# Down projection of a fused Hyena filter and gated layer with the tokens held in the array and the weights moving

## The chip, the cores and the metric

The kernel runs on one core of a Trainium2 chip. The metric is the device time of one execution in microseconds (us); lower is better. About 0.2% (7.5 us) is what a measurement of this kernel can tell from no change.

## The reference

Everything is float32. A long convolution of each of 128 channels over 12480 positions is followed by a layer on 49920 tokens of width 128 with 2048 hidden units:

```
u = x * v                                   # (4, 12480, 128)
h_filt = (relu(pos_emb @ w1) @ w2) * exp(-0.01 * pos)[:, None]
y = causal convolution of u with h_filt, channel by channel (rfft, product, irfft)
z = (x * y).reshape(49920, 128)
h = z @ w_in                                # (49920, 2048)
g = h * cos(h)
return g @ w_out                            # (49920, 128)
```

The change lies in the last line, `g @ w_out`, the down projection, whose inner size is 2048.

## The kernel before

The convolution is done as a transform in two factors, 96 by 120, with matmuls against tables (the lines L407, L448, L479 and L504 are its four kinds of matmul). It leaves z in DRAM in rows of four tokens. The gated layer (named "moe" in the code) takes z back in tiles `n` of up to 128 rows, so of up to 512 tokens: there are 98 tiles, the first with 104 rows, the last with 88, the 96 between with 128. Each tile goes through 16 pieces `c` of 128 hidden units.

One step `(n, c)` has these parts. `moe_up` (L743) multiplies piece `c` of `w_in`, held in the array, with the tile's 512 tokens as the moving operand, into a PSUM bank `ph` of which there are four. ACT (L746), DVE (L749), POOL (L752), ACT (L757) and DVE (L759) turn `ph` into `gt = h * cos(h)`, laid out with the 128 hidden units on the partitions and the 512 tokens along the row. `moe_down` (L768) multiplies piece `c` of `w_out`, held in the array, with `gt` as the moving operand, and adds into the bank `acc`, whose rows are the 128 output features. After piece 15 `moe_evict` copies `acc` to `ot` (L774, on ACT). Since the sums stand with features on the partitions, `moe_back` turns them with four transposes on TensorE (L126, through a `ph` bank) and copies the result to `ob` (L783, on ACT), and `moe_store` issues the DMAs to the output from SP's queue (L794). `moe_turn` does the same kind of four transposes on the way in, from `zb` to `at` (L126, L737).

The order of all of it is written out by hand in one loop. In iteration `i`, which is step `(n, c)`, the loop issues the up projection of step `i`, the down projection of step `i - 4` (`LAG = 4`), the evict if that was a piece 15, the second half of the gating of step `i - 1`, and then by the value of `c`: the turn of the next tile at `c = 3`, the way back of the tile before at `c = 8`, its store at `c = 10`. After that it issues as many units of the next batch's convolution as are owed, so that the convolutions of batches 1 to 3 and the last part of batch 0's lie between the steps; at about 3000 us there is no convolution left and the steps stand alone.

For reading the trace: every float32 matmul that is no transpose appears as two weight loads and two matmul records, so a step's up projection is "x2" and its down projection is "x2". A transpose appears as one weight load and one matmul record.

Of the kernel before, what the change touches and what calls it, by code (L numbers as in the profile page):

```python
# [9 lines left out]
F32 = mybir.dt.float32  # L10
# [6 lines left out]
P = 128  # L17
BANK = 512
# [12 lines left out]
def kernel(  # L31
# [46 lines left out]
    nc = tc.nc  # L78

    B, S, D = x.shape  # L80
# [18 lines left out]
    NFC = DFF // P  # L99
    G = BANK // D  # L100
    UA = 2
# [4 lines left out]
    LAG = 4  # L106
# [17 lines left out]
    def transpose(dst, src, ident):  # L124
        n = src.shape[0]
        nc.tensor.transpose(dst, src, ident[0:n, 0:n])  # L126
# [241 lines left out]
    def n2s(g):  # L368

        a = g * UA  # L370
        return [*range(a, a + UA), *range(N2 - UA - a, N2 - a)]
# [344 lines left out]
    ats, accs = {}, {}  # L716

    def first_row(n):
        return min(R + (n - 1) * P, NROWS) if n else 0

    def rows_of(n):
        return first_row(n + 1) - first_row(n)
# [7 lines left out]
    def moe_turn(pool, n):  # L730
        m = rows_of(n)
        zb = zbs.pop(n)
        pt = ps_h.tile([P, BANK], F32, name="ph")
        for i in range(G):
            transpose(pt[:, i * m:(i + 1) * m], zb[0:m, i, :], ident)
        at = pool.tile([D, BANK], F32, name="at")
        nc.scalar.copy(out=at[:, 0:G * m], in_=pt[:, 0:G * m])  # L737
        ats[n] = at

    def moe_up(pool, n, c):  # L740
        m = G * rows_of(n)
        ph = ps_h.tile([P, BANK], F32, name="ph")
        nc.tensor.matmul(ph[:, 0:m], w_in_sb[:, c * P:(c + 1) * P], ats[n][:, 0:m],  # L743
                         start=True, stop=True)
        a = pool.tile([P, BANK], F32, name="a", bufs=3)
        nc.scalar.activation(a[:, 0:m], ph[:, 0:m], AF.Identity,  # L746
                             bias=quarter[:, 0:1], scale=INV_TWO_PI)
        k = pool.tile([P, BANK], F32, name="k")
        nc.vector.tensor_scalar(out=k[:, 0:m], in0=a[:, 0:m], scalar1=ROUND,  # L749
                                scalar2=ROUND, op0=ALU.add, op1=ALU.subtract)  # L750
        f = pool.tile([P, BANK], F32, name="f")
        nc.gpsimd.tensor_tensor(f[:, 0:m], a[:, 0:m], k[:, 0:m], op=ALU.subtract)  # L752
        return ph, f, m

    def moe_act(pool, ph, f, m):
        cs = pool.tile([P, BANK], F32, name="cs")
        nc.scalar.activation(cs[:, 0:m], f[:, 0:m], AF.Sin, scale=TWO_PI)  # L757
        gt = pool.tile([P, BANK], F32, name="gt", bufs=4)
        nc.vector.tensor_tensor(gt[:, 0:m], ph[:, 0:m], cs[:, 0:m], op=ALU.mult)  # L759
        return gt  # L760

    def moe_down(n, c, gt):
        if c == 0:

            accs[n] = bank() if made[0] == B * NG and n % 2 else \
                ps_acc.tile([P, BANK], F32, name="acc")
        m = G * rows_of(n)
        nc.tensor.matmul(accs[n][:, 0:m], w_out_sb[:, c, :], gt[:, 0:m],  # L768
                         start=(c == 0), stop=(c == NFC - 1))

    def moe_evict(pool, n):
        m = G * rows_of(n)
        ot = pool.tile([D, BANK], F32, name="ot", bufs=1)
        nc.scalar.copy(out=ot[:, 0:m], in_=accs.pop(n)[:, 0:m])  # L774
        return ot

    def moe_back(pool, n, ot):
        m = rows_of(n)
        pt = ps_h.tile([P, BANK], F32, name="ph")
        for i in range(G):  # L780
            transpose(pt[0:m, i * D:(i + 1) * D], ot[:, i * m:(i + 1) * m], ident)
        ob = pool.tile([P, 2, UA * D], F32, name="ob", bufs=1)
        nc.scalar.copy(out=ob[0:m, :, :].rearrange("p h n -> p (h n)"), in_=pt[0:m, :])  # L783
        return ob

    def moe_store(n, ob):
        row = first_row(n)
        while row < first_row(n + 1):
            b, g, n1 = row // R // NG, row // R % NG, row % R
            count = min(R - n1, first_row(n + 1) - row)  # L790
            first, _, second, _ = n2s(g)
            start = out[b * S + n1 * N2 + first, :]
            at = row - first_row(n)
            nc.sync.dma_start(  # L794
                bass.AP(tensor=start.tensor, offset=start.offset,
                        ap=[[N2 * D, count], [(second - first) * D, 2], [1, UA * D]]),
                ob[at:at + count, :, :])
            row += count

    with tc.manual_schedule():  # L800
        with tc.tile_pool(name="psum", bufs=8, space=PSUM) as psum, \
                ExitStack() as first:
            def bank():
                return psum.tile([P, BANK], F32, name="ps")
# [11 lines left out]
            with tc.tile_pool(name="layers", bufs=1, side="right") as pool:  # L816
# [14 lines left out]
                ident = pool.tile([P, P], F32, name="ident")  # L831
# [68 lines left out]
            ident = wpool.tile([P, P], F32, name="ident")  # L900
            make_identity(nc, ident)
            w_in_sb = wpool.tile([D, DFF], F32, name="w_in_sb")
            w_out_sb = wpool.tile([P, NFC, D], F32, name="w_out_sb")
# [6 lines left out]
        ps_h = ctx.enter_context(tc.tile_pool(name="ps_h", bufs=4, space=PSUM))  # L910
# [9 lines left out]
        mpool = ctx.enter_context(tc.tile_pool(name="moe", bufs=2))  # L920
# [18 lines left out]
        def load(n):  # L939
            while made[0] * R < first_row(n + 1):  # L940
                next(conv)
            moe_load(mpool, n)
# [2 lines left out]
            next(conv)  # L945
        moe_turn(mpool, 0)
        steps = [(n, c) for n in range(NALL) for c in range(NFC)]
        hidden, gates, ots, obs = {}, {}, {}, {}
        for i in range(len(steps) + LAG):
            if i < len(steps):  # L950
                n, c = steps[i]
                if n == 0 and c == NFC // 2:
                    load(1)
                if c == NFC - 4 and n + 2 < NALL:
                    load(n + 2)
                hidden[i] = moe_up(mpool, n, c)
            if i >= LAG:
                pn, pc = steps[i - LAG]
                moe_down(pn, pc, gates.pop(i - LAG))
                if pc == NFC - 1:  # L960
                    ots[pn] = moe_evict(mpool, pn)
            if 0 <= i - 1 < len(steps):
                gates[i - 1] = moe_act(mpool, *hidden.pop(i - 1))
            if i < len(steps):

                if c == (LAG - 1 if n else NFC - 2) and n + 1 < NALL:
                    moe_turn(mpool, n + 1)
                if c == NFC // 2 and n - 1 in ots:
                    obs[n - 1] = moe_back(mpool, n - 1, ots.pop(n - 1))
                if c == NFC // 2 + 2 and n - 1 in obs:  # L970
                    moe_store(n - 1, obs.pop(n - 1))
            owed += 1.0
            while owed > 0.0:
                owed -= next(conv, owed)
        for n in sorted(ots):
            moe_store(n, moe_back(mpool, n, ots[n]))
# [1 line left out]
_INS = ['x', 'v', 'pos_emb', 'w1', 'w2', 'moe_w_in', 'moe_w_out']  # L978
_OUTS = [((49920, 128), 'float32')]
# [25 lines left out]
```

## Time and profile before

| what | value |
|---|---|
| median of 3 runs | 3759.47 us (3757.68 to 3761.73) |
| profiled execution: span | 3758.9 us |
| instructions in the span | 47177 |
| mean granted TensorE clock | 0.995 |
| PE busy, matmuls | 3690.6 us, 98% of the span, 13546 records |
| PE weight loads (PEld), beside the matmuls | 2110.4 us, 56% |
| DVE, ACT, POOL busy | 74%, 67%, 68% |

The profiled execution's span lies 0.6 us below the median of the runs, within their spread. In the trace an operation is named by engine, line and tiles, as `acc<-gt,w_out_sb 128*128 128x512` for a matmul that writes `acc`, has a stationary operand of 128 by 128 and a moving one of 128 by 512. Matmul and weight-load records have modelled ends that include the way through the array, so that successive records overlap: how long one occupies TensorE is read from the distance between successive starts, not from a record's length.

### The profile page before, as it was taken

Reading aid. Unit: us, or ns where it says so; the run is one execution under the profiler, and the core shown is the slowest. Engines: PE = TensorE matmul, PEld = TensorE weight load, DVE = VectorE, ACT = ScalarE, POOL = GpSimd, SP = SyncE. Lnnn points to the kernel's source line nnn. Section 1 sums busy time; section 2 is a strip of 40 time slices with the busy share of each in tenths; the row PEclk is TensorE's granted clock in tenths of the full one; section 3 lists DMA queues with packets and bytes.
Section 4 is the critical chain, followed back from the end, with each engine's and each line's share of the span. In section 5 each row is a group of like instructions: output and inputs, shape, how many; then the busy total and the mean of one; then the engine's idle time right before and its main releaser. Section 6 shows DMA issues by size and latency. Waiting matters only on the chain.

```text
span 3758.9 us, 47177 instructions
## 1 busy us (share of the span) xinstructions
PE 3690.6 (98%) x13546; PEld 2110.4 (56%) x13546; DVE 2773.7 (74%) x5586; ACT 2508.2 (67%) x4660; POOL 2557.6 (68%) x2318
## 2 busy tenths in 40 slices
PE   7898999999999999999999999999999999999999
PEld 6777555555566556555565556555566544444444
DVE  8887997687866787788766776788765666666666
ACT  5757776766665557766665567666664677777777
POOL 6666776588845665688745664788644677777776
PEclk9999999999999999999999999999999999999999
DMA  6263551022203650122104530122105200000000
GB/s 167 64 185 107 155 167 33 25 72 79 72 12 91 181 151 12 40 79 77 52 18 128 180 105 21 52 79 76 38 21 172 76 23 17 17 23 18 17 23 13
DMA packets 209499, 276.14 MB, mean 73 GB/s; under 512 B 17111, under 2 KB 146535, under 8 KB 209111
## 3 DMA queue, kind: packets, MB, share of 16 engines
q1 hardware_dynamic: 209239, 273.12, 24.8%
q8 instruction: 109, 1.79, 0.2%
q14 instruction: 151, 1.24, 0.1%
HBM read 193.64 MB, written 79.42 MB: 73 GB/s over the span
## 4 chain that ended last, share of the span: by engine, by line
PE 88%; DVE 3%; POOL 3%; ACT 2%; DMA 2%; issue 1%; SPq 0%; POOLq 0%; DVEq 0%; ACTq 0%
PE ph L743 33%; PE acc L768 28%; PE cv L504 5%; PE cv L768 5%; PE cv L479 4%; PE cv L407 3%; PE cv L448 3%; PE ph L126 2%; POOL f L752 1%; PE ps L407 1%; PE ps L448 1%; DMA tm<-td 1%; DMA wd<-w 1%; ACT cs L757 1%; DVE k L749 1%
## 5 line engine op out<-in xcount | busy, mean ns | idle before, releaser
L752 POOL TENSOR_TENSOR f<-a,k 128x512 f32<-128x512 f32 (+1 forms) x1568 | 1986.2, 1267 | 1060.5 <-DVE k L749 1059.1
L743 PE MATMUL ph<-at,w_in_sb 128*128 128x512 f32 (+1 forms) x3136 | 1599.0, 591 | 3.7 <-DVE gt L759 2.7
L746 ACT ACTIVATE a<-ph,quarter 128x512 f32<-128x512 f32 (+1 forms) x1568 | 1071.2, 683 | 704.8 <-PE ph L743 695.2
L768 PE MATMUL acc<-gt,w_out_sb 128*128 128x512 f32 (+1 forms) x2688 | 1370.3, 591 | 0.0
L759 DVE TENSOR_TENSOR gt<-ph,cs 128x512 f32<-128x512 f32 (+1 forms) x1568 | 1077.3, 687 | 359.9 <-ACT cs L757 341.8
L757 ACT ACTIVATE cs<-f 128x512 f32<-128x512 f32 (+1 forms) x1568 | 981.0, 626 | 366.6 <-POOL f L752 364.3
L749 DVE TENSOR_SCALAR k<-a 128x512 f32<-128x512 f32 (+1 forms) x1568 | 792.9, 506 | 550.7 <-ACT a L746 524.2
L768 PEld LDWEIGHTS acc<-gt,w_out_sb 128*128 128x128 f32 x2688 | 508.4, 189 | 642.8 <-issue 631.9
L743 PEld LDWEIGHTS ph<-at,w_in_sb 128*128 128x128 f32 x3136 | 553.2, 190 | 337.7 <-issue 257.5
L474 POOL TENSOR_TENSOR slots<-slots,t 120x256 f32<-120x256 f32 x384 | 312.9, 821 | 59.9 <-DVE t L467 25.6
L504 PEld LDWEIGHTS cv<-slots,tm 96*104 96x104 f32 x1920 | 238.6, 169 | 106.8 <-issue 85.4
L504 PE MATMUL cv<-slots,tm 96*104 96x128 f32 x1920 | 251.7, 273 | 9.9 <-POOL tm L297 5.0
L768 PE MATMUL cv<-gt,w_out_sb 128*128 128x512 f32 (+1 forms) x448 | 224.5, 583 | 1.0 <-DVE gt L759 1.0
L479 PEld LDWEIGHTS cv<-cs,slots 120*96 120x96 f32 x1536 | 176.7, 167 | 67.2 <-issue 65.2
L479 PE MATMUL cv<-cs,slots 120*96 120x120 f32 x1536 | 183.2, 266 | 0.0
L448 PEld LDWEIGHTS cv<-slots,w 124*120 124x120 f32 x576 | 103.7, 184 | 124.3 <-issue 112.3
L407 PEld LDWEIGHTS cv<-c,slots 104*124 104x124 f32 x768 | 132.6, 192 | 72.2 <-issue 60.0
L448 PE MATMUL cv<-slots,w 124*120 124x256 f32 x576 | 173.0, 380 | 0.0
L407 PE MATMUL cv<-c,slots 104*124 104x192 f32 x768 | 151.8, 327 | 5.4 <-DVE gt L759 3.5
L768 PEld LDWEIGHTS cv<-gt,w_out_sb 128*128 128x128 f32 x448 | 84.9, 190 | 104.8 <-issue 99.5
L489 DVE TENSOR_TENSOR slots<-cv,other 96x240 f32<-96x240 f32 x384 | 133.1, 394 | 1.5 <-ACT other L487 1.4
L395 DVE TENSOR_TENSOR xt<-xt,vt 104x256 f32<-104x256 f32 x177 | 132.6, 751 | 0.6 <-DMA vt<-in_v_dram 0.6
(131 smaller groups left out, 2520.9 us busy)
## 6 DMA issues: line engine op xcount, KB each, us to landing
h<-hd SPq DMA_DIRECT2D x144, 240.0 KB
tm<-td SPq DMA_DIRECT2D x96, 312.0 KB
xt<-in_x_dram SPq DMA_DIRECT2D x120, 208.0 KB
vt<-in_v_dram SPq DMA_DIRECT2D x120, 208.0 KB
xs<-in_x_dram SPq DMA_DIRECT2D x120, 208.0 KB
zd<-zs SPq DMA_DIRECT2D x119, 208.0 KB
zb<-zd SPq DMA_DIRECT2D x96, 256.0 KB
w<-wd SPq DMA_DIRECT2D x144, 116.2 KB
```

The source lines that it names most:

```text
L407: nc.tensor.matmul(ps[0:KE, i * 2 * N1:(i + 1) * 2 * N1], u[:, b, 0:KE, i], c1[0:u.shape[0], :, :].rearrange("p r k -> p (r k)"), start=Tr ...
L448: nc.tensor.matmul(pi, w[:, i, :], parts[0:KE, :, k], start=True, stop=True)
L474: nc.gpsimd.tensor_tensor(y[:, r], y[:, r], t[:, r], op=op)
L479: nc.tensor.matmul(ps[0:N1, (i * 2 + r) * N2:(i * 2 + r + 1) * N2], parts[0:N2, r, :, b, i], cs[:, r, :], start=True, stop=True)
L504: nc.tensor.matmul(ps[0:R, i * D:(i + 1) * D], t[:, i, r, :], slots[0:N1, :, place, :], start=(r == 0), stop=(r == 1))
L743: nc.tensor.matmul(ph[:, 0:m], w_in_sb[:, c * P:(c + 1) * P], ats[n][:, 0:m], start=True, stop=True)
L746: nc.scalar.activation(a[:, 0:m], ph[:, 0:m], AF.Identity, bias=quarter[:, 0:1], scale=INV_TWO_PI)
L749: nc.vector.tensor_scalar(out=k[:, 0:m], in0=a[:, 0:m], scalar1=ROUND, scalar2=ROUND, op0=ALU.add, op1=ALU.subtract)
L752: nc.gpsimd.tensor_tensor(f[:, 0:m], a[:, 0:m], k[:, 0:m], op=ALU.subtract)
L757: nc.scalar.activation(cs[:, 0:m], f[:, 0:m], AF.Sin, scale=TWO_PI)
L759: nc.vector.tensor_tensor(gt[:, 0:m], ph[:, 0:m], cs[:, 0:m], op=ALU.mult)
L768: nc.tensor.matmul(accs[n][:, 0:m], w_out_sb[:, c, :], gt[:, 0:m], start=(c == 0), stop=(c == NFC - 1))
```

## The change

`moe_down` swaps its operands. The 128 hidden units by `m` tokens of `gt` are held in the array (`m` is the tile's number of rows, 128 in all but two tiles), four pieces one after the other, and `w_out`'s piece of 128 by 128 moves. Its sums come out with tokens on the partitions, `G = 4` column blocks of 128 features in one bank. One copy takes them to `ob`; `moe_back`, `ot`, the four transposes and the second copy are gone. `ob` has two buffers where it had one, and the store is issued at `c = 6` instead of 10.

```diff
-        m = G * rows_of(n)
-        nc.tensor.matmul(accs[n][:, 0:m], w_out_sb[:, c, :], gt[:, 0:m],
-                         start=(c == 0), stop=(c == NFC - 1))
+        m = rows_of(n)
+        for i in range(G):
+            nc.tensor.matmul(accs[n][0:m, i * D:(i + 1) * D], gt[:, i * m:(i + 1) * m],
+                             w_out_sb[:, c, :], start=(c == 0 and i == 0),
+                             stop=(c == NFC - 1), skip_group_check=True)
 
     def moe_evict(pool, n):
-        m = G * rows_of(n)
-        ot = pool.tile([D, BANK], F32, name="ot", bufs=1)
-        nc.scalar.copy(out=ot[:, 0:m], in_=accs.pop(n)[:, 0:m])
-        return ot
-
-    def moe_back(pool, n, ot):
         m = rows_of(n)
-        pt = ps_h.tile([P, BANK], F32, name="ph")
-        for i in range(G):
-            transpose(pt[0:m, i * D:(i + 1) * D], ot[:, i * m:(i + 1) * m], ident)
-        ob = pool.tile([P, 2, UA * D], F32, name="ob", bufs=1)
-        nc.scalar.copy(out=ob[0:m, :, :].rearrange("p h n -> p (h n)"), in_=pt[0:m, :])
+        ob = pool.tile([P, 2, UA * D], F32, name="ob")
+        nc.scalar.copy(out=ob[0:m, :, :].rearrange("p h n -> p (h n)"),
+                       in_=accs.pop(n)[0:m, :])
         return ob
...
                 if pc == NFC - 1:
-                    ots[pn] = moe_evict(mpool, pn)
+                    obs[pn] = moe_evict(mpool, pn)
...
-                if c == NFC // 2 and n - 1 in ots:
-                    obs[n - 1] = moe_back(mpool, n - 1, ots.pop(n - 1))
-                if c == NFC // 2 + 2 and n - 1 in obs:
+                if c == LAG + 2 and n - 1 in obs:
                     moe_store(n - 1, obs.pop(n - 1))
...
-        for n in sorted(ots):
-            moe_store(n, moe_back(mpool, n, ots[n]))
+        for n in sorted(obs):
+            moe_store(n, obs[n])
```

More of the change, by code (lines that the diff above doesn't have):

```diff
@@ L947 @@
         steps = [(n, c) for n in range(NALL) for c in range(NFC)]
-        hidden, gates, ots, obs = {}, {}, {}, {}
+        hidden, gates, obs = {}, {}, {}
         for i in range(len(steps) + LAG):
```

## The prediction

> **What bounds the kernel now.** I read the page first: which engine is full, and which lines make the chain that ended last.
>
> ```profile
> PE 3690.6 (98%) x13546; PEld 2110.4 (56%) x13546; DVE 2773.7 (74%) x5586; ACT 2508.2 (67%) x4660; POOL 2557.6 (68%) x2318
> PE 88%; DVE 3%; POOL 3%; ACT 2%; DMA 2%; issue 1%; SPq 0%; POOLq 0%; DVEq 0%; ACTq 0%
> ```
>
> TensorE is busy for 98% and makes 88% of the chain. A busy PE proves little, since the ends of its records are modelled, so I looked at its starts in the stage without convolution, with the view in order of time of PE alone, where a row merges records that touch.
>
> ```profile
> 3035.59 0.59 PE L768 MATMUL acc<-gt,w_out_sb 128*128 128x512 f32 x1
> 3036.01 0.60 PE L126 MATMUL ph<-ident,ot 128*128 128x128 f32 x4
> 3036.45 1.02 PE L743 MATMUL ph<-at,w_in_sb 128*128 128x512 f32 x2
> ```
>
> From one way back to the next the trace shows 28.345 us, ten times running. The parts add up to that: 64 records of 512 columns at 428.7 to 430.4 ns from start to start (medians over the trace 429 to 431) are 27.46 us, and 8 transposes at 109.2 ns are 0.87. Nothing is left over: TensorE works without a hole, and any nanosecond added to or taken from its stream shows in the end. In the table by stretches of 200 us, PE's busy time falls short of the stretch by 18 us in all from 400 us on, 6 of them in the last 159 us. So the forecast is a sum over TensorE's stream.
>
> **What goes.** Per full tile, four transposes of `ot`: four starts at 109.2 ns (mean distance of 576 successive L126 records) are 437 ns; in the rows above, 3036.45 - 3036.01 = 0.44. In 96 tiles 41.9 us. The second ACT copy (0.574 us x 98) lies beside TensorE, ACT being idle for a fifth of the stage without convolution, and is worth nothing before the end. A `ph` bank less is taken per tile; PE's waits for DVE's `gt` at L743 are 2.7 us in all, so that is the most it can give.
>
> **What comes.** Old down step: 2 records of 512 columns, 857.6 ns. New: 4 matmuls of 128 moving columns, so 8 records with 8 weight loads in front. The same 1024 columns flow; the question is what a record of 128 columns with a new 128-column load behind it occupies. Call it r. A full tile changes by 16 x (8r - 857.6) - 437 ns, zero at r = 110.6 ns. No single row has this shape, but two rows bound its two halves.
>
> The moving half: fp32 records of 120 contiguous columns (L479) start 102.6 ns apart, in one run of 257 records too, so neither issue nor fetching sets a limit there; 120 columns at the 0.833 ns that 512 take (428.7 - 2.1, over 512) are 100, and 2.6 stay. For 128 columns this gives 106.7 + 2.6 = 109.3; the transposes' 109.2 is the same. L504 and L454 (128 columns, two floats at a time) take 111.3 and 110.6, but their moving operand is strided, and L448, strided with 256 columns, is 5 ns over L357, which is contiguous. `w_out_sb[:, c, :]` is contiguous.
>
> The loading half: an fp32 load of 128 columns behind short matmuls exists, that of L743 after a run of convolution.
>
> ```profile
> 2673.98 0.99 PE L479 MATMUL cv<-cs,slots 120*96 120x120 f32 x8
> 2674.80 1.03 PE L743 MATMUL ph<-at,w_in_sb 128*128 128x512 f32 x2
> ```
> ```profile
> 2673.98 0.79 PEld L479 LDWEIGHTS cv<-cs,slots 120*96 120x96 f32 x7 [0.26 <-issue]
> 2674.70 0.30 PEld L743 LDWEIGHTS ph<-at,w_in_sb 128*128 128x128 f32 x2
> 2675.24 0.19 PEld L768 LDWEIGHTS acc<-gt,w_out_sb 128*128 128x128 f32 x1 [0.24 <-issue]
> ```
>
> A load starts 2 ns after the matmul before it starts, so load and matmul run side by side. The merged pair of 0.30 us less the 0.19 of one says that the second load comes 0.11 after the first. Over the trace that distance is 109.9 ns (155 times, p10 to p90 110) where the matmul in front needs only 102.6, and 109.8 after a transpose (92 times): the load itself takes 109.9, just over the 109.3 of the moving half. Where the moving half is slower, after L504, it is 111.8.
>
> So r is the later of 109.3 and 109.9. Two limits so close may add a little: after L504 the sum was 0.5 over the larger (111.3 to 111.8). I take 110.2, and keep 109.2 (loads that hide in a chain better than singly) and 111.8 (both limits felt as after L504) as ends. Full tiles: 16 x (8 x 110.2 - 857.6) - 437 = -53 ns, times 96 = -5.1 us, and 12.3 us for each ns of r.
>
> The two short tiles lose something that is easily missed: `w_out` always moves 128 columns, whatever the rows. First tile (416 moving columns before): 2 x 348.5 = 697 becomes 8 x 109.3 = 874, 16 steps, +2.8, less 0.44 for its transposes: +2.4 us. Last tile (352): 2 x 295.5 = 591 becomes 874, +0.283 in about 13 steps (the last three wait for `gt` and have room): +3.7 us.
>
> The end: after the last matmul the trace has a copy, the transposes, a second copy and the store.
>
> ```profile
> 3753.76 0.45 ACT L774 COPY ot<-cv 128x352 f32<-128x352 f32 x1 [1.51 <-PE cv L768]
> 3754.26 0.39 PEld L126 LDWEIGHTS ph<-ident,ot 128*88 128x88 f32 x4 [1.10 <-ACT ot L774]
> 3754.27 0.64 PE L126 MATMUL ph<-ident,ot 128*88 128x128 f32 x4 [0.54 <-ACT ot L774]
> 3754.94 0.58 ACT L783 COPY ob<-ph 88x512 f32<-88x512 f32 x1 [0.73 <-PE ph L126]
> ```
>
> The 0.58 us copy will start where the first one did: 3754.94 - 3753.76 = 1.2 us less.
>
> Sum: -5.1 + 2.4 + 3.7 - 1.2 = -0.2 us on the span of 3758.9; put on the median of the runs, 0.6 higher, 3759.3 us. The saving of the transposes is paid out again in 2 ns per record.
>
> **Edits taken at nothing, and their cover.** `gt` is now awaited by a weight load, a record earlier than the matmul that awaited it. In the last stage it is ready 1.9 us or more before its load (0.5 us at the least before 3740 us); if that were gone each step would wait with the up projection of the next steps queued behind it. The evict keeps its place in ACT's order; behind it TensorE has at least an up projection of 0.86 us before it needs the bank, against 0.58 us of copy and about 0.2 of hand-over, and in the next iteration four transposes more; without that cover a tile would lose at most the copy, 0.58 us, 57 us in 98. The store moves from c = 10 to c = 6 in SP's queue, ahead of the `zb` load at c = 12 and of some convolution loads. It waits for the evict issued at c = 3, so SP holds what is behind it for fewer steps than before; PE's waits for `tm<-td` total 4.8 us, which bounds gain or loss. PE gets 12 x 1568 - 784 = 18000 more records; L479's run of 257 pairs, 51 ns a record, shows that the rate holds.
>
> The rows above show a load 2 ns behind its predecessor's start. The Trainium skill, TensorE: Matmul & The Clock Gate, "Part 3: Packing small matmuls", states that a weight load overlaps a running matmul only when the row group differs. By that rule a record would cost 109.9 + 109.3 ns, a down step 1754, and the estimate from it is 1.4 ms more; the trace contradicts it here, for full-height loads.
>
> **Rivals.** *Faster:* loads hide wholly and the moving half alone sets r = 109.2. For it: transposes with 128-column loads run so. Against: those loads are shorter records (141 ns against 190), and the fp32 load showed its own 109.9. It gives -0.2 - 12.3 = 3747 us. *Slower:* the chain of loads that have no slack picks up the two limits' jitter, as after L504: from r = 110.8 on it is over the bound, at 111.8 it is +19.7, 3779 us. For it: each of the eight loads has 0.6 ns or less to give, and nothing in the trace runs a chain of eight with both limits equal; against it: the 110 after L479 hardly scatters. *Nothing to remove:* if the transposes had lain in holes the whole price of r = 110.2 would stand (16 x 24 ns x 96 = 36.9, 6.5 in the short tiles, less 1.2), 3802; the period that adds up speaks against it.
>
> **How the numbers follow.** r between 109.6 and 110.8 is within 7.5 us, the 0.2% that a measurement of this kernel can tell: 0.50, own range 3752 to 3767. Faster, r below 109.6: 0.14. Slower, r above 110.8: 0.36, of which 0.04 for the cases beyond 3779. Ends at 3747 and 3779 leave out less than 2 in 10.
>
> **What would show it.** In the last stage the period of a tile should be 28.29 us instead of 28.345; L768 stands as x8 rows 0.88 us before the next L743; the L126 rows with `ot` and L783 after an `ot` are gone; PEld's share rises, POOL's and DVE's busy times stay. A period over 28.37, or under 28.22, decides for a rival; holes of PE in front of L768 would say that a wait I priced at nothing is real.

## The result, and the profile after

The changed kernel takes 3765.62 us (median of 20 runs, 3763.1 to 3769.07) beside 3759.69 us for the kernel before in the same comparison: ratio 1.0015, 95% interval 1.0008 to 1.0022. It is 5.9 us slower, where 3759.3 us, 0.2 under the median of before, was forecast: inside the range of the forecast (3747 to 3779) and less than 0.2%, but with 20 runs of each kernel clear of scatter. The profiled execution spans 3764.1 us, 5.2 more than before.

The page of the changed kernel, its engine line and its chain:

```profile
PE 3702.4 (98%) x22562; PEld 2890.1 (77%) x22562; DVE 2760.1 (73%) x5586; ACT 2469.0 (66%) x4562; POOL 2558.3 (68%) x2318
PE 90%; DVE 3%; DMA 3%; POOL 2%; ACT 1%; issue 1%; SPq 0%; DVEq 0%; ACTq 0%; POOLq 0%
```

TensorE bounds it as before. Its busy time rose by 11.8 us (3690.6 to 3702.4), the span only by 5.2: TensorE is idle for 61.7 us (3764.1 - 3702.4) where it was idle for 68.3. So the stream got dearer by more than the result shows, and less idle time makes up the difference.

The same stretch without convolution, in order of time, first PE, then its weight loads:

```profile
3440.53 1.05 PE L769 MATMUL acc<-w_out_sb,gt 128*128 128x128 f32 x8
3441.42 1.02 PE L743 MATMUL ph<-at,w_in_sb 128*128 128x512 f32 x2
3442.28 1.05 PE L769 MATMUL acc<-w_out_sb,gt 128*128 128x128 f32 x8
```
```profile
3440.53 0.86 PEld L769 LDWEIGHTS acc<-w_out_sb,gt 128*128 128x128 f32 x7 [0.24 <-issue]
3441.31 0.30 PEld L743 LDWEIGHTS ph<-at,w_in_sb 128*128 128x128 f32 x2
3441.85 0.19 PEld L769 LDWEIGHTS acc<-w_out_sb,gt 128*128 128x128 f32 x1 [0.24 <-issue]
```

The step takes 1.75 us from one L769 row to the next; it took 1.716. The down projection's eight records take 0.89 us up to the next L743 row, not the 0.88 of the forecast. From the start times one by one, the middle intervals between matmuls in such a run are 111.6 ns, not 110.2. A tile of this stage takes 28.463 us (28.345 before): +0.118 us where -0.053 was forecast. The granted clock of this stretch is 1.00 in both traces.

The end, in order of time: the transposes and the second copy are gone.

```profile
3755.63 4.53 PE L769 MATMUL cv<-w_out_sb,gt 128*88 128x128 f32 x40
3760.20 0.58 ACT L776 COPY ob<-cv 88x512 f32<-88x512 f32 x1 [1.83 <-PE cv L769]
3760.81 0.31 SPq L788 DMA_DIRECT2D out_dram<-ob  x1
```

Where the 5.2 us of the two spans arise, from the starts of the tiles' first up projections in both traces:

| stretch | change, us |
|---|---|
| up to the first step | -0.3 |
| first tile | +1.8 |
| tiles 1 to 69, convolution between the steps | -0.5 |
| tiles 70 to 96, no convolution | +3.2 |
| last tile to the end | +0.95 |

Two things ask for a cause: why a record takes 111.6 ns, and why 69 tiles that cost 0.1 us more each when nothing disturbs them (33.18 to 33.28 us, for instance) end up no longer in sum.

### The profile page after: what moved, and what is told of

Its sections match the earlier page's. It is cut to its first block, busy times and chain, and to the rows that moved or that the text cites. A ratio compares the mean times of both kernels' runs of the same rounds, so it can differ in the third digit from the quotient of the medians.

```text
span 3764.1 us, 65120 instructions
## 1 busy us (share of the span) xinstructions
PE 3702.4 (98%) x22562; PEld 2890.1 (77%) x22562; DVE 2760.1 (73%) x5586; ACT 2469.0 (66%) x4562; POOL 2558.3 (68%) x2318
## 4 chain that ended last, share of the span: by engine, by line
PE 90%; DVE 3%; DMA 3%; POOL 2%; ACT 1%; issue 1%; SPq 0%; DVEq 0%; ACTq 0%; POOLq 0%
PE ph L743 34%; PE acc L769 30%; PE cv L769 5%; PE cv L504 5%; PE cv L479 4%; PE cv L448 3%; PE cv L407 3%; PE ph L126 1%; PE ps L407 1%; POOL f L752 1%; PE ps L479 1%; DMA tm<-td 1%; PE ps L448 1%; DMA hd<-h 1%; DMA wd<-w 1%
## 5 line engine op out<-in xcount | busy, mean ns | idle before, releaser
L769 PEld LDWEIGHTS acc<-w_out_sb,gt 128*128 128x128 f32 (+1 forms) x10752 | 1408.3, 191 | 642.4 <-issue 630.3
L743 PE MATMUL ph<-at,w_in_sb 128*128 128x512 f32 (+1 forms) x3136 | 1598.7, 591 | 1.3 <-DVE gt L759 0.7
L746 ACT ACTIVATE a<-ph,quarter 128x512 f32<-128x512 f32 (+1 forms) x1568 | 1073.1, 684 | 780.2 <-PE ph L743 772.2
L769 PE MATMUL acc<-w_out_sb,gt 128*128 128x128 f32 (+1 forms) x10752 | 1415.7, 275 | 0.0
L749 DVE TENSOR_SCALAR k<-a 128x512 f32<-128x512 f32 (+1 forms) x1568 | 780.1, 498 | 575.9 <-ACT a L746 558.6
L743 PEld LDWEIGHTS ph<-at,w_in_sb 128*128 128x128 f32 x3136 | 504.1, 191 | 22.9 <-DVE gt L759 1.3
L769 PEld LDWEIGHTS cv<-w_out_sb,gt 128*128 128x128 f32 (+1 forms) x1792 | 233.6, 189 | 102.3 <-issue 99.4
L504 PEld LDWEIGHTS cv<-slots,tm 96*104 96x104 f32 x1920 | 227.9, 169 | 9.9 <-POOL tm L297 5.2
L769 PE MATMUL cv<-w_out_sb,gt 128*128 128x128 f32 (+1 forms) x1792 | 235.2, 275 | 0.0
L479 PE MATMUL cv<-cs,slots 120*96 120x120 f32 x1536 | 183.1, 266 | 0.0
L479 PEld LDWEIGHTS cv<-cs,slots 120*96 120x96 f32 x1536 | 169.1, 167 | 0.0
L407 PEld LDWEIGHTS cv<-c,slots 104*124 104x124 f32 x768 | 122.2, 193 | 7.3 <-POOL slots L401 4.1
L471 DVE TENSOR_TENSOR slots<-cv,h 120x256 f32<-120x256 f32 x288 | 119.3, 414 | 0.0
```

The costliest lines, as they stand in the source:

```text
L407: nc.tensor.matmul(ps[0:KE, i * 2 * N1:(i + 1) * 2 * N1], u[:, b, 0:KE, i], c1[0:u.shape[0], :, :].rearrange("p r k -> p (r k)"), start=Tr ...
L479: nc.tensor.matmul(ps[0:N1, (i * 2 + r) * N2:(i * 2 + r + 1) * N2], parts[0:N2, r, :, b, i], cs[:, r, :], start=True, stop=True)
L504: nc.tensor.matmul(ps[0:R, i * D:(i + 1) * D], t[:, i, r, :], slots[0:N1, :, place, :], start=(r == 0), stop=(r == 1))
L746: nc.scalar.activation(a[:, 0:m], ph[:, 0:m], AF.Identity, bias=quarter[:, 0:1], scale=INV_TWO_PI)
L769: nc.tensor.matmul(accs[n][0:m, i * D:(i + 1) * D], gt[:, i * m:(i + 1) * m], w_out_sb[:, c, :], start=(c == 0 and i == 0), stop=(c == NFC ...
```

## The experiments

### What sets the distance between short matmuls

One run of the changed kernel, with a different size in every two tiles of the last stage (a setting of `load` columns of `gt` and `move` columns of `w_out` in pieces 1 to 15):

```diff
+            load, move = m, D
+            if c > 0 and 72 <= n < 96:
+                load, move = SIZES[(n - 72) // 2]
+                if load == 0:
+                    load = 96 if i % 2 else 128
-            nc.tensor.matmul(accs[n][0:m, i * D:(i + 1) * D], gt[:, i * m:(i + 1) * m],
-                             w_out_sb[:, c, :], start=(c == 0 and i == 0),
+            nc.tensor.matmul(accs[n][0:load, i * D:i * D + move], gt[:, i * m:i * m + load],
+                             w_out_sb[:, c, 0:move], start=(c == 0 and i == 0),
```

> The changed kernel, in which tiles 72 to 95 (two tiles for each setting, in the stage without convolution) load fewer columns of gt or move fewer columns of w_out in pieces 1 to 15; what is not loaded or moved is left out of the sums. Settings (load, move): 128/128, 126/128, 124/128, 120/128, 112/128, 64/128, 128/124, 128/120, 128/112, 128/96, 128/64, and 128 and 96 loaded by turns with 128 moving. Read is the distance r between successive starts. My theory, two nearly equal limits (load 109.9 ns, matmul 109.3) that in a chain add up to 111.6: r falls to 109.2 to 109.5 as soon as the load is 124 columns or less, and falls to 109.9 as soon as 124 columns or fewer move. Rival, a load of 128 columns in a chain costs 111.6 by itself: r stays at 111.6 for 124 down to 64 moving columns, and falls 0.83 ns per column of load until the matmul's 109.2. Rival, the sums in PSUM or the issue set r: it stays at 111.6 for every load and falls with the moving columns.

PE in order of time, in three of the settings (the down projection is L777, the up projection L746 in this kernel):

```profile
3069.42 1.05 PE L777 MATMUL cv<-w_out_sb,gt 128*128 128x128 f32 x8
3070.31 0.59 PE L746 MATMUL ph<-at,w_in_sb 128*128 128x512 f32 x1
...
3238.98 1.04 PE L777 MATMUL cv<-w_out_sb,gt 128*120 128x128 f32 x8
3239.85 0.59 PE L746 MATMUL ph<-at,w_in_sb 128*128 128x512 f32 x1
...
3475.53 1.05 PE L777 MATMUL cv<-w_out_sb,gt 128*128 128x120 f32 x8
3476.41 0.60 PE L746 MATMUL ph<-at,w_in_sb 128*128 128x512 f32 x1
```

Eight columns less to load shorten the run of eight from 0.89 to 0.87 us; eight columns less to move leave it at 0.88. The mean of the middle intervals, from the trace's start times:

| load / move | r, ns | | load / move | r, ns |
|---|---|---|---|---|
| 128/128 | 111.67 | | 128/124 | 111.67 |
| 126/128 | 110.00 | | 128/120 | 111.67 |
| 124/128 | 109.17 | | 128/112 | 111.67 |
| 120/128 | 109.17 | | 128/96 | 111.67 |
| 112/128 | 109.17 | | 128/64 | 111.67 |
| 64/128 | 109.17 | | 128 and 96 by turns/128 | 110.44 |

My theory falls and the rival holds: there is no adding-up of two near limits. A load of 128 columns costs 111.67 ns in a chain whatever moves beside it, down to 64 columns; two columns less take 1.67 ns off, 0.833 each, until the matmul's own 109.17 is reached. Load and matmul run beside each other, and the longer one counts: the load is its columns at 0.833 ns and 5.0 more (from the two sizes that bind, 128 and 126), the matmul its columns at 0.833 and 2.5 more (at 128; the first distance of a run, whose load was taken ahead, is 105.9, 102.7, 95.8, 82.3 and 55.8 ns for 124, 120, 112, 96 and 64 columns). The issue is excluded, since the number of records is the same in all of the settings, and so are the sums written to PSUM, which halve from 128/128 to 128/64 while r stays.

The setting by turns also shows where a load's time stands in the trace. Of its eight distances the first is 109.0 (its load was taken ahead); behind the other three matmuls with 128 columns loaded it is 111.7, behind the four with 96 it is 109.0 to 109.3, whatever the next one loads. So the wait for a load stands behind the start of the matmul that uses it, not before it.

The whole kernel with shorter loads gives what that is worth (120 columns in pieces 1 to 15 of the full tiles):

```diff
+        load = 120 if m == P and c > 0 else m
-            nc.tensor.matmul(accs[n][0:m, i * D:(i + 1) * D], gt[:, i * m:(i + 1) * m],
+            nc.tensor.matmul(accs[n][0:load, i * D:(i + 1) * D], gt[:, i * m:i * m + load],
```

> The changed kernel with 120 instead of 128 columns of gt loaded in pieces 1 to 15 of the 96 full tiles (8 tokens of each 128 are left out of those sums); all else, 128 moving columns, number of instructions, the order, is the same. My theory, the load sets r: r goes from 111.3 to 109.2, 96 x 15 x 8 x 2.1 = 24 us less, of which waits give some back: 3741 to 3745 us. Rival, r comes from issue, from the sums in PSUM or from SBUF being shared: 3764 to 3767 us, no change.

It took 3746.78 us beside 3761.16 for the kernel before, ratio 0.9961 (0.9948 to 0.9973): 14.4 us under it, so some 20 under the changed kernel (3766.88 us when it was run again, below), and 1.8 us over what theory had said. The tile of the last stage takes 28.201 us instead of 28.463: 0.262, times 96 is 25.2 us. The load is confirmed as the cause of r; and of 25 us only 20 arrive. What is missing lies between the convolution's steps: in tiles 1 to 69 of the two traces 18.1 us were due (69 x 0.262) and 9.5 came. The page's engine line:

```profile
PE 3678.3 (98%) x22562; PEld 2852.9 (76%) x22562; DVE 2775.1 (74%) x5586; ACT 2461.7 (66%) x4562; POOL 2563.5 (68%) x2318
```

With a span of 3745.4 us TensorE is idle for 67.1 us, 5.4 more than in the changed kernel.

### What the removal alone is worth

The kernel before, its full tiles copied once and stored as they stand, features on the partitions:

```diff
+        if m == BANK:
+            ob = pool.tile([P, 2, UA * D], F32, name="ob", bufs=1)
+            nc.scalar.copy(out=ob[:, :, :].rearrange("p h n -> p (h n)"), in_=accs.pop(n)[:, :])
+            return ob
```

> The kernel before with the way back left out in the 96 full tiles: the sums are copied once, with features on the partitions, and stored so (the output is not turned). What the removal alone is worth. My theory, TensorE's stream has no holes and the four transposes cost 0.437 us a tile: 96 x 0.437 = 42 us less, 3716 to 3719 us. Rival, waits on other engines and DMAs in the stages with convolution give part of it back: 3721 us or more, with PE's idle time after 400 us up from 14 us to 18 or more.

It took 3730.54 us beside 3761.16, ratio 0.9916 (0.9902 to 0.9929): 30.6 us less, not 42. In the stage without convolution the sum holds to the nanosecond: a tile takes 27.906 us, 0.439 less, and 27 tiles give 11.9 us. In tiles 1 to 69 it should have been 30 and was 18.0. The engine line of the page, and of the list of waits two lines of the kernel before and the same two of this one:

```profile
PE 3654.7 (98%) x13162; PEld 2070.7 (56%) x13162; DVE 2787.5 (75%) x5586; ACT 2445.6 (66%) x4564; POOL 2561.3 (69%) x2318
```
```profile
PE cv L504 <- DMA tm<-td: 4.8, 6, 1.4
PE ph L743 <- DVE gt L759: 2.7, 5, 0.8
```
```profile
PE ph L743 <- DVE gt L759: 6.3, 11, 1.4
PE cv L504 <- DMA tm<-td: 5.7, 6, 1.5
```

TensorE's idle time is 74.3 us (3729.0 - 3654.7), 6.0 more than before, and its waits for `gt` at L743 (2.7 us before) and for `tm` (4.8) both grew. Part of the 12 us that are missing does not show as idle: some tiles in the transform's second stage take 33.0 to 33.5 us where their neighbours take 32.74 and the kernel before took 33.18. POOL is busy there for 88% (116.6 of 133 us), which makes it a candidate for a second bound; that was not tested.

So the rival holds: waits on other engines and DMAs end at their own time, and a faster stream meets more of them. That a slower one meets fewer would explain the changed kernel, but this run does not show it. There 10 us of dearer steps were due (69 x 0.098 and 27 x 0.118); the 3.2 us of the last 27 tiles arrive in full, and of the 6.8 of the other 69 nothing (-0.5). The store moved in the same change, so it has to be asked what the store did.

### Whether the earlier store had a part in it

Four variants of the changed kernel move the store or take a buffer away, and the changed kernel itself was run again:

```diff
-                if c == LAG + 2 and n - 1 in obs:
+                if c == NFC // 2 + 2 and n - 1 in obs:      # c = 10; c = NFC - 2 = 14 in another
-        ob = pool.tile([P, 2, UA * D], F32, name="ob")
+        ob = pool.tile([P, 2, UA * D], F32, name="ob", bufs=1)   # in two of them
```

> The changed kernel with the store back at c = 10 and one buffer for ob. My theory, the idle time that TensorE lost against the sum (some 7 us less than before the change) is lost because TensorE comes later to waits that end at their own time, and the store has no part in it: within 1.5 us of the changed kernel, 3764 to 3767 us. Rival, the earlier store lets SP's queue issue the convolution's loads earlier and that gave the 4 us: 3769 to 3770 us, with PE's waits for tm back at 4 to 5 us.

> The changed kernel again, unaltered, so that the place of the store and the number of ob buffers are compared on one chip. All theories: 1.0015 of the kernel before, some 3766 us beside 3760.

> The changed kernel with one buffer for ob, the store staying at c = 6. Theory, the place of the store in SP's queue made the 4 us between the changed kernel and the one with the store at c = 10: within 1.5 us of the changed kernel. Rival, the second buffer made them: 3 to 5 us over the changed kernel, PE's waits for tm at 4 to 6 us.

> The changed kernel with the store at c = 10 and its two ob buffers kept, on the same chip as the store at c = 14. Theory: 8 to 10 us over the kernel before, PE's waits for tm at 4 us or more. Rival: 5 to 7 us over it, as the changed kernel.

> The changed kernel with the store at c = 14, behind the load of zb at c = 12, two ob buffers. Theory, the place of the store in SP's queue sets how late the convolution's loads are: the effect grows with the distance, so 8 to 14 us over the kernel before on the same chip, where the changed kernel is 6 over it, with PE's waits for tm over 6 us. Rival, the 3 us between c = 6 and c = 10 were scatter: 5 to 7 us over the kernel before.

| store at c | ob buffers | over the kernel before, us | ratio (95% interval) | tiles 1 to 69, us |
|---|---|---|---|---|
| 6, the changed kernel again | 2 | 5.9 | 1.0017 (1.0008 to 1.0026) | -1.5 |
| 6 | 1 | 7.0 | 1.0018 (1.0009 to 1.0027) | -1.5 |
| 10 | 2 | 7.0 | 1.0019 (1.0010 to 1.0028) | +1.4 |
| 10 | 1 | 8.8 | 1.0025 (1.0015 to 1.0034) | +5.2 |
| 14 | 2 | 6.8 | 1.0017 (1.0007 to 1.0026) | +1.7 |

The run with the store at 10 and one buffer was made first. Its 3769.92 us lie where its rival had put them, which seemed to say that the store's place was worth 3 us, and its PE waits for `tm` are the longest of the five. The list of waits, of that kernel and of the one with the store at 10 and two buffers:

```profile
PE cv L504 <- DMA tm<-td: 5.8, 9, 2.1
```
```profile
PE cv L504 <- DMA tm<-td: 3.4, 9, 0.7
```

The store at 14 shows that the effect does not grow with the distance, and all intervals overlap: the times separate neither the place nor the second buffer from nothing.

The traces, one of each, lean the other way. With the store at 6 four of them (the changed kernel twice, the kernel of the map, which is the same up to tile 71, and the one with one buffer) put tiles 1 to 69 at -1.5 to -0.5 us, with the store at 10 or 14 three put them at +1.4 to +5.2. TensorE's idle time in these tiles is 6.7 to 8.4 us in the four, 9.4 to 11.8 in the three and 12.4 in the kernel before. The run at 10 with one buffer differs from the kernel before in nothing but the orientation and the way back that it makes needless; there 5.2 of the 6.8 us due arrive, and idle time falls by only 0.6. So what became of the extra cost in the changed kernel's tiles 1 to 69 stays open: in part or whole it may be the earlier store that paid it. The prediction's "nothing" for this edit is not refuted by the times, but the traces suggest 2 to 3 us with two buffers and 7 with one.

The other side of the question, the way back and the store moved forward in the kernel before:

```diff
-                if c == NFC // 2 and n - 1 in ots:
+                if c == LAG and n - 1 in ots:
...
-                if c == NFC // 2 + 2 and n - 1 in obs:
+                if c == LAG + 2 and n - 1 in obs:
```

> The kernel before with its way back at c = 4 instead of 8 and its store at c = 6 instead of 10; orientation, transposes and buffers as before. Theory, the earlier store is worth some 4 us of waits for tm and has nothing to do with the orientation: 3 to 5 us under the kernel before, which would beat both kernels. Rival, in the kernel before the transposes at c = 4 come right behind the turn of the next tile at c = 3 and make the up projections wait for a ph bank: 0 to 5 us over the kernel before, PE's waits for gt at L743 over 3 us.

3757.93 us beside 3761.0, ratio 0.9992 (0.9983 to 1.0001): 3 us less, not clear of scatter, with PE's waits for `tm` down from 4.8 to 1.1 us and its idle time in tiles 1 to 69 from 12.4 to 9.1. It points the same way: the earlier store seems to be worth some 3 us in either orientation.

```profile
PE cv L504 <- DMA tm<-td: 1.1, 3, 0.5
```

### A version that beats both

The removal is worth 31 us if the sums can be turned elsewhere. VectorE turns blocks of 32 by 32; what it leaves needs stores of 32 floats at a time:

```diff
+        if m == BANK:
+            nc.vector.transpose(ot[:, :], accs.pop(n)[:, :])
+            return ot
...
+                    for q in range(D // SQ):
+                        for h in range(2):
+                            nc.sync.dma_start(
+                                bass.AP(tensor=there.tensor,
+                                        offset=there.offset + q * SQ + h * (second_ - first_) * D,
+                                        ap=[[N2 * D, rows], [D, UA], [1, SQ]]),
+                                blocks[q * SQ + t:q * SQ + t + rows, h, :, r, :])
```

> The kernel before in which the 96 full tiles are turned by VectorE in blocks of 32 by 32, from the bank to ot, in place of ACT's copy, TensorE's four transposes and ACT's second copy; the store writes runs of 32 floats, some 40 DMAs a tile. Theory, this keeps what leaving out the way back was worth (31 us): 3730 to 3737 us, faster than both kernels. Rival, 196000 writes of 128 bytes and the many issues on SP's queue delay the loads of the convolution: 3750 us or more, with PE waiting for tm, xt and h for tens of us.

4353.33 us, ratio 1.1575 (1.1559 to 1.159): the rival, and far worse than it said. The list of waits:

```profile
PE cv L449 <- DMA w<-wd: 281.1, 25, 17.4
PE cv L505 <- DMA tm<-td: 190.7, 14, 19.9
```

The convolution's loads come too late by hundreds of microseconds, on the queue that now has some 40 issues a tile before them; whether the number of issues or the narrow writes delay them was not separated. The granted clock is 0.929 in this run (0.995 before), so a slower TensorE is part of the loss. But in the stage without convolution a tile took 27.905 us, the full saving. Two versions use it only where nothing is loaded, or little (with the early way back and store elsewhere):

```diff
+BLOCKED = {7, 8, 9, 19, 20, 29, 30, 41, 42, 51, 52, 63, 64, *range(69, 97)}   # one version
+BLOCKED = range(69, 97)                                                       # the other
-        if m == BANK:
+        if blocked(n):      # n in BLOCKED and rows_of(n) == P
```

> The kernel before with the early way back and store (c = 4 and c = 6), and 41 of its full tiles turned by VectorE in blocks of 32 by 32 with stores of 32 floats: the 28 tiles of the stage without convolution and 13 in the stages in which the convolution loads little. Theory, there SP and the DMA engines have room and each such tile saves its 0.44 us: 41 x 0.44 = 18 under the early version, 3740 to 3744 us beside 3761, faster than both kernels. Rival, the many issues spill into the next loading stage: between 3745 and 3765 us, the tiles after the 13 longer by several us.

> The same with only the 28 tiles of the stage without convolution turned by VectorE. Theory: 28 x 0.44 = 12 us under the early version, 3745 to 3748 us beside 3761. Rival, the block turn or the narrow store delays something of the steps there too: the period of a tile stays above 28.0 us and the time above 3750 us.

With 41 tiles 3752.88 us, ratio 0.9979 (0.9970 to 0.9988): the rival. But its trace shows the spill in one place only. Tile 10, behind the turned tiles 7 to 9, takes 42.69 us instead of 34.91, with a wait of 6.0 us for a load; beside the version with 28 tiles, twelve tiles are shorter by 0.44 us each, 5.3 in all. So the turned tiles pay there too, and one badly placed group takes more than all of it back. The line of the list of waits:

```profile
PE cv L451 <- DMA w<-wd: 6.0, 1, 6.0
```

With the 28 last tiles 3749.17 us beside 3761.85, ratio 0.9971 (0.9959 to 0.9982): 12.7 us faster than the kernel before, the fastest of those that leave nothing out. The time lies between what theory and rival said: a tile takes 27.906 us as forecast, but the last tile's evict waits 6.6 us for `ot`, still being stored in narrow pieces:

```profile
3742.71 0.45 ACT L783 COPY ot<-cv 128x352 f32<-128x352 f32 x1 [6.57 <-DMA out_dram<-ot]
```

A second `ot` buffer, or leaving the last full tile to TensorE, should take that away; it was not tried, and neither was the version with 41 tiles less its tiles 7 to 9.

## Why the prediction was right or wrong

**The loading half of r: the step that failed.** I priced a load of 128 columns at 109.9 ns from the distance between the starts of two load records of L743, and so put r at 110.2. In a chain the load costs 111.67, and r is 111.6. That load and matmul run side by side and the later one counts was right; the load's price was not. The trace of before held the right number in the same places, one reading away: the record of a matmul that waits for its weights starts before it moves anything, and the wait shows in the distance to the next matmul. After a transpose, L743's second record came 109 + 432 = 541 ns after the transpose's start; less the 428.7 of an undisturbed record this is 112.3 for the short matmul with the load behind it, and 112.3 after L479 too. The prediction went by the load starts instead, which understate the first load of a series by 2 ns: in the changed kernel the load starts say 109.4 for the first short one, the matmul starts 111.3. With r = 111.6 the prediction's own formula gives 16 x (8 x 111.6 - 857.6) - 437 = +127 ns for a full tile; +118 was measured.

**"Every nanosecond shows in the end": right for 27 tiles, wrong for 69.** The argument was a tile period that adds up, taken from the stage without convolution and used for all stages. There it held in each variant. Between the convolution's steps 40% or more of a gain is taken up by waits that do not move with TensorE: in tiles 1 to 69, 8.6 of 18.1 us with short loads and 12.3 of 30.3 with the way back left out. Of the 6.8 us that the change should have cost there none arrives; whether waits or the earlier store took them stays open. With r right and this step as it was, the forecast would have been -0.2 + 12.3 x 1.4 = +17 us, too slow; the two errors are of opposite sign. So it is luck that the forecast is off by only 6 us, and that the time lies in its own range, that of r from 109.6 to 110.8, while r itself is that of the slower rival.

**The removed transposes** were 0.439 us of a tile against 0.437 forecast. **The short tiles:** the last one took 2.4 us more up to its last up projection, with the 0.44 us of the transposes of the tile before gone from it, where +3.7 was forecast without them; after that 1.4 us were saved, not 1.2. Its sum is +0.95 where +2.5 was forecast. The first tile's +2.4 can't be seen: it varies from 29.5 to 31.7 us over these runs, in either orientation.

**Edits taken at nothing:** the wait of the load for `gt`, the evict and the number of records cost nothing that shows: the last 27 tiles have no hole of TensorE in either trace. The store is treated above; its part is open.

**The rivals.** The faster one, loads wholly hidden, is refuted: they are longer than the matmuls. The slower one named 111.8 for r, which is the size that came, but by jitter of two limits, which the widths refute. Nothing to remove is refuted by the period of 27.906.

**The rule of the Trainium skill** that a load overlaps a matmul only in another row group (TensorE: Matmul & The Clock Gate, "Part 3: Packing small matmuls") does not hold for these full-height loads: a distance of 111.6 ns holds a load of 111.67 and a matmul of 109.17 each time.

## What to carry to other kernels

When operands are swapped so that the short side moves, the price here was set by the longer of load and matmul. With 128 columns on both sides of a float32 matmul that is the load, by 2.5 ns a record; the new down projection has 12544 records, and loads shorter by 8 columns in most of them gave 20 us. Read the price of a load from how late the matmul after it comes, its second record included, not from the distance between the loads. And check a "stream without holes" in every stage: a period that adds up in one stage says nothing on another, where waits that end at their own time keep part of what is won. And an edit that rides along, as the earlier store did, needs a run of its own before a difference is put down to the main one.

## What was not expected of the hardware

A load of 64 columns was not taken ahead of a running matmul with 128 columns loaded. All engines in order of time, in the setting 64/128:

```profile
3326.39 1.12 PE L746 MATMUL ph<-at,w_in_sb 128*128 128x512 f32 x2
...
3327.44 0.85 PEld L777 LDWEIGHTS acc<-w_out_sb,gt 128*64 128x64 f32 x8 [0.76 <-issue]
3327.44 1.09 PE L777 MATMUL acc<-w_out_sb,gt 128*64 128x128 f32 x8
```

The first of the eight loads starts 1.05 us after the up projection's start, 0.07 us before its row ends, where a load of 96 columns or more starts under it. The same holds the other way: from the last of the eight, with 64 columns loaded, to the up projection, which loads 128, it is 202.5 ns instead of 109.2. A step takes 2.07 us instead of 1.75, although r within the run is 109.17. Loads of 112 and of 96 columns showed nothing of the kind. Why, no run shows.
